# A block-sparse attention and gated FFN kernel: V rows of 96 halves instead of 66, and output slots of 128 words instead of 66

## The chip, the cores and the metric

The kernel runs on one core of one Trainium2 chip. The metric is device time in microseconds (us); a profile's span, from the first to the last recorded instruction, is about 2 us shorter. A run counts as slow when it is over 1.5% above the fastest run of the same kernel; all runs told of here are fast, or are single runs of a kernel (state unknown, since one run has nothing to be compared with).

## The reference, cut to what matters

```
# q, k, v: (4 batches, 8 heads, 768 tokens, 64)
scores = scale * np.matmul(q, k.transpose(0, 1, 3, 2))
scores = np.where(mask, scores, -1000000000.0)          # mask by blocks of 32 tokens
attn = np.exp(scores - max); attn = attn / (sum + 1e-09)
attn_out = np.matmul(attn, v)
x = attn_out as (3072 tokens, 512)
out = (sigmoid(x @ w_gate) * (x @ w_val)) @ w_out       # 512 -> 1536 -> 512
```

(The softmax and sigmoid lines are shortened.) The change concerns `attn @ v` alone.

## The kernel before: the parts that matter

A program of operations is ordered ahead of time by a small scheduler, so each engine gets a fixed list. V is held as eight tiles, each with rows for two heads and six key blocks of 128 keys. A row has 64 values of one key as halves (16-bit floating-point numbers, two bytes each), and then ones: the 65th column of the product is the sum of the weights, by which the output is divided.

```python
VW = 66
...
vring = [one([128, 2, NJ, VW], f16, f"v16_{i}") for i in range(8)]       # NJ = 6
...
lambda i=i: nc.vector.memset(vring[i]()[:, :, :, 64:VW], 1.0),           # the ones, once
...
lambda: nc.vector.tensor_copy(t()[:, :, :, 0:64], s()),                  # cast_v: the values
...
o, rz, x16 = psb([4, VW]), sb("rz", [128, 4, 1], f32), sb("x16", [128, 2, 128], f16)

def values():                                                            # L681 in the profile
    v_ = v16[b, p]()
    for jq in range(2):
        for hd in range(2):
            for j in range(NJ):
                nc.tensor.matmul(
                    o()[:, 2 * jq + hd, 0:65],
                    pts[j // 2]()[:, hd, j % 2, jq * 128 : jq * 128 + 128],
                    v_[:, hd, j, 0:65],
                    start=(j == 0), stop=(j == NJ - 1),
                )
...   # then, on VectorE: L691 rz = 1 / o[:, :, 64:65], L695 x16 = o[:, :, 0:64] * rz
```

`values` is a burst of 24 matmuls, and there are 48 bursts. Each matmul has its own weight load (of `pts`, the exponentials) and streams one row of the V tile, 65 columns, through it. `psb([4, VW])` takes a bank of PSUM, the memory that the products go to, and lays the four output slots of a burst at steps of VW words of four bytes.

The softmax here doesn't subtract the row's maximum and nothing guards it: scores larger than these inputs give would overflow.

## Time and profile before

| what | value | where from |
|---|---|---|
| time | 292.51 us (291.97 to 293.05, four runs) | timed runs |
| TensorE busy | 98% of 290.6 us | table of busy times |
| ScalarE, VectorE busy | 70%, 64% | the same |
| a burst of 24 V matmuls, start to next work | 0.76 us, 31.7 ns a matmul | timeline of PE |
| one of these matmuls in the group table | 193 ns | groups by line |

The last two rows differ because matmuls overlap.

### The profile page before, as it was taken

How to read it: one execution, taken by the hardware profiler on the slowest of the kernel's cores; microseconds unless marked ns; L12 is line 12 of the kernel's file. 1: busy time of each engine (PE TensorE's matmuls, PEld its weight loads, DVE VectorE, ACT ScalarE, POOL GpSimd, SP SyncE). 2: the span in 40 equal slices, each digit the busy share in tenths (PEclk: the TensorE clock that was granted, in tenths of full speed). 3: DMA queues.
4: the chain of work that ended last, by engine and by line, in shares of the span. 5: the costliest groups of instructions: out<-in, count | busy, mean ns of one | idle time of the engine just before them, and what ended most of it. 6: DMA issues, size and time to landing. Idle time of an engine off the chain costs nothing.

```text
span 290.6 us, 7279 instructions
## 1 busy us (share of the span) xinstructions
PE 285.1 (98%) x3030; PEld 175.1 (60%) x3030; DVE 186.5 (64%) x401; ACT 204.4 (70%) x281; POOL 14.8 (5%) x24
## 2 busy tenths in 40 slices
PE   7998999999999999999999999999999999999995
PEld 6676786687578655555554555555555555447753
DVE  3587997898897876867486576476476565223210
ACT  2878888987898898886898796776777673333321
POOL 8740000000000000000000000000000000000000
PEclk9999999999999999999999999999999999999999
DMA  7999998993799973051957651011011011000013
GB/s 106 175 208 210 208 252 229 237 276 65 217 199 210 218 206 64 18 182 25 224 171 165 211 89 56 9 49 54 11 47 54 11 46 56 36 36 35 9 67 111
DMA packets 50785, 35.25 MB, mean 121 GB/s; under 512 B 31376, under 2 KB 47808, under 8 KB 50752
## 3 DMA queue, kind: packets, MB, share of 16 engines
q1 hardware_dynamic: 43304, 27.71, 36.8%
q0 software_dynamic: 7232, 7.01, 15.0%
q8 instruction: 23, 0.38, 0.5%
q10 hardware_dynamic: 216, 0.07, 0.1%
q14 instruction: 10, 0.08, 0.1%
HBM read 28.42 MB, written 6.29 MB: 119 GB/s over the span
## 4 chain that ended last, share of the span: by engine, by line
PE 96%; ACT 2%; DMA 1%; ACTq 0%; issue 0%
PE psum L746 44%; PE psum L791 22%; PE psum L640 14%; PE psum L681 12%; ACT pt L658 1%; PE psum L457 1%; DMA e<-bb_e 1%; PE psum L380 1%; PE psum L720 1%; PE psum L602 1%; PE psum L578 0%; ACTq L353 0%; ACTq L357 0%; ACT y L809 0%; ACTq L658 0%
## 5 line engine op out<-in xcount | busy, mean ns | idle before, releaser
L658 ACT ACTIVATE pt<-psum 128x1024 f16<-128x1024 f32 x144 | 138.9, 1029 | 26.3 <-PE psum L640 26.3
L666 DVE TENSOR_TENSOR pt<-pt,mask 128x1024 f16<-128x1024 f16 x132 | 88.5, 687 | 45.9 <-ACT pt L658 45.8
L746 PE MATMUL psum<-x,wv 128*128 128x256 f16 (+1 forms) x384 | 78.2, 326 | 0.0
L746 PE MATMUL psum<-x,wg 128*128 128x256 f16 (+1 forms) x384 | 78.1, 326 | 0.0
L767 ACT ACTIVATE tg<-psum 128x256 f32<-128x256 f32 (+1 forms) x96 | 47.5, 499 | 42.6 <-PE psum L746 31.8
L791 PE MATMUL psum<-wo,h 128*128 128x512 f16 (+2 forms) x300 | 73.0, 371 | 0.0
L774 DVE SCALAR_TENSOR_TENSOR h<-tg,psum 128x256 f16<-128x256 f32 (+1 forms) x96 | 52.3, 551 | 29.1 <-PE psum L746 16.1
L746 PEld LDWEIGHTS <-wg 128*128 128x128 f16 x384 | 36.0, 98 | 24.3 <-issue 1.7
L746 PEld LDWEIGHTS <-wv 128*128 128x128 f16 x384 | 35.3, 98 | 23.0 <-issue 2.5
L681 PEld LDWEIGHTS <-pt 128*128 128x128 f16 x1152 | 42.5, 98 | 8.8 <-issue 1.1
L640 PE MATMUL psum<-qT,kT 64*128 64x256 f16 x576 | 46.0, 274 | 0.5 <-ACT pt L658 0.4
L791 PEld LDWEIGHTS <-h 128*128 128x128 f16 x300 | 26.4, 98 | 30.2 <-issue 5.7
L681 PE MATMUL psum<-v,pt 128*128 128x65 f16 x1152 | 44.3, 193 | 0.3 <-ACT pt L658 0.3
L640 PEld LDWEIGHTS <-kT 64*128 64x128 f16 x576 | 24.9, 95 | 18.5 <-issue 15.2
L695 DVE TENSOR_TENSOR x<-psum,rz 128x256 f16<-128x256 f32 x48 | 20.4, 424 | 1.8 <-DVE rz L691 0.2
L809 ACT ACTIVATE y<-psum 128x512 f32<-128x512 f32 (+2 forms) x22 | 12.7, 579 | 11.0 <-PE psum L791 10.8
L691 DVE RECIPROCAL rz<-psum 128x4 f32<-128x4 f32 x48 | 8.6, 179 | 5.5 <-PE psum L681 5.4
L380 PE MATMUL psum<-zero 128*64 128x128 f16 x44 | 6.4, 294 | 1.0 <-DVE zero L350 1.0
L640 PE MATMUL psum<-bias,e 64*128 64x256 f16 x48 | 7.1, 307 | 0.0
L427 ACT CAST q<-qs 128x768 f16<-128x768 f32 x8 | 6.8, 844 | 0.0
L610 DVE TENSOR_SCALAR mask<-psum 128x512 f16<-128x512 f32 x9 | 6.0, 683 | 0.5 <-PE psum L640 0.5
L380 PEld LDWEIGHTS <-zero 128*64 128x64 f16 x44 | 4.7, 159 | 2.3 <-issue 1.3
(54 smaller groups left out, 73.1 us busy)
## 6 DMA issues: line engine op xcount, KB each, us to landing
out_dram<-y SPq DMA_DIRECT2D x23, 256.0 KB, 2.0
qs<-in_q_dram SPq DMA_DIRECT2D x12, 384.0 KB, 4.5
vs<-in_v_dram SPq DMA_DIRECT2D x12, 384.0 KB, 4.9
ks<-in_k_dram SPq DMA_DIRECT2D x12, 384.0 KB, 4.4
wg<-in_moe_w_gate_dram POOLq DMA_DIRECT2D x2, 768.0 KB, 13.1
wv<-in_moe_w_val_dram POOLq DMA_DIRECT2D x2, 768.0 KB, 15.8
wo<-in_moe_w_out_dram POOLq DMA_DIRECT2D x3, 512.0 KB, 21.9
vh<-in_v_dram POOLq DMA_DIRECT2D x4, 192.0 KB, 7.7
```

What stands on the lines that cost most here:

```text
L380: "PE", dur, lambda: nc.tensor.matmul(t()[0:64], zero()[:, 0:64], zero(), start=True, stop=True),
L640: nc.tensor.matmul(st()[:, hd, jj * CH : (jj + 1) * CH], l[r, 2 * tt + jj, :], m[r, 2 * c : 2 * c + 2, :], start=not (own and masked), sto ...
L658: lambda st=st, pt=pt: nc.scalar.activation(pt().rearrange("p h j q -> p h (j q)"), st(), AF.Exp, scale=SCALE),
L666: nc.vector.tensor_tensor(t, t, mask()[:, c, tt].unsqueeze(1).to_broadcast([128, 2, 512]), op=ALU.mult)
L681: nc.tensor.matmul(o()[:, 2 * jq + hd, 0:65], pts[j // 2]()[:, hd, j % 2, jq * 128 : jq * 128 + 128], v_[:, hd, j, 0:65], start=(j == 0), ...
L691: "DVE", 0.2, lambda: nc.vector.reciprocal(rz(), o()[:, :, 64:65]), reads=[o], writes=[rz], prio=seq - 5
L695: lambda: nc.vector.tensor_tensor(x16().rearrange("p j (h d) -> p (j h) d", d=64), o()[:, :, 0:64], rz().to_broadcast([128, 4, 64]), op=AL ...
L746: nc.tensor.matmul(t()[:, z : z + w], wt()[:, i, f * 128 : (f + 1) * 128], xT[g, i]()[:, 0:w], start=(i == 0), stop=(i == NP - 1),)
L767: lambda tg=tg, a=pair[0]: nc.scalar.activation(tg()[:, 0:w], a[0]()[:, a[1] : a[1] + w], AF.Tanh, scale=0.5),
L774: lambda tg=tg, a=pair[1], h_=h_: nc.vector.scalar_tensor_tensor(h_()[:, 0:w], tg()[:, 0:w], 1.0, a[0]()[:, a[1] : a[1] + w], op0=ALU.add, ...
L791: nc.tensor.matmul(py()[:, m], hts[g, f]()[:, tt * 128 : (tt + 1) * 128], wo()[:, f, m], start=(f == 0), stop=(f == NF - 1),)
L809: lambda py=py, y=y, m=m: nc.scalar.activation(y()[:, m], py()[:, m], AF.Copy, scale=0.5),
```

## The change

A change of alignment: rows of 96 halves are 192 bytes, so every row starts at a multiple of 64 bytes within its tile; and the four slots of 128 words (512 bytes) lie each on a 512-byte boundary. The whole diff:

```diff
-VW = 66
+VW = 96
...
-            lambda i=i: nc.vector.memset(vring[i]()[:, :, :, 64:VW], 1.0),
+            lambda i=i: nc.vector.memset(vring[i]()[:, :, :, 64:65], 1.0),
...
-        o, rz, x16 = psb([4, VW]), sb("rz", [128, 4, 1], f32), sb("x16", [128, 2, 128], f16)
+        o, rz, x16 = psb([4, 128]), sb("rz", [128, 4, 1], f32), sb("x16", [128, 2, 128], f16)
```

## The prediction

> **What bounds the kernel now.** I read the page's table of busy times first, then the chain that ended last, then the groups by line, then the timeline of one steady stretch, and at the end the start times of single matmuls in the trace. The table of busy times says which engine is full:
>
> ```profile
> PE 285.1 (98%) x3030; PEld 175.1 (60%) x3030; DVE 186.5 (64%) x401; ACT 204.4 (70%) x281; POOL 14.8 (5%) x24
> ```
>
> TensorE (PE) is busy 98% of 290.6 us, and no other engine passes 70%. The chain of work that ended last says whether the end hangs on it:
>
> ```profile
> PE 96%; ACT 2%; DMA 1%; ACTq 0%; issue 0%
> PE psum L746 44%; PE psum L791 22%; PE psum L640 14%; PE psum L681 12%; ACT pt L658 1%; PE psum L457 1%; DMA e<-bb_e 1%; PE psum L380 1%; PE psum L720 1%; PE psum L602 1%; PE psum L578 0%; ACTq L353 0%; ACTq L357 0%; ACT y L809 0%; ACTq L658 0%
> ```
>
> 96% of the span is matmul after matmul on PE. The change touches one line of these, L681, the product of attention weights and values: 12% of the span, about 36 us (the chain in order of time gives 12.5%, 36.3 us). The groups by line show how many such matmuls there are, and what reads their result:
>
> ```profile
> L681 PEld LDWEIGHTS <-pt 128*128 128x128 f16 x1152 | 42.5, 98 | 8.8 <-issue 1.1
> L681 PE MATMUL psum<-v,pt 128*128 128x65 f16 x1152 | 44.3, 193 | 0.3 <-ACT pt L658 0.3
> L695 DVE TENSOR_TENSOR x<-psum,rz 128x256 f16<-128x256 f32 x48 | 20.4, 424 | 1.8 <-DVE rz L691 0.2
> L691 DVE RECIPROCAL rz<-psum 128x4 f32<-128x4 f32 x48 | 8.6, 179 | 5.5 <-PE psum L681 5.4
> ```
>
> 1152 matmuls are 48 bursts of 24: two query halves by two heads by six key blocks. Each needs its own weight load and streams 65 columns of the V tile (64 values and a one that sums the weights). A mean of 193 ns is no cost: 1152 x 193 would be 222 us, and the group is busy for 44.3. What counts is how far apart they start. The timeline of PE in a steady stretch gives that by burst:
>
> ```profile
> 188.56 0.92 PE L681 MATMUL psum<-v,pt 128*128 128x65 f16 x24
> 189.32 1.02 PE L746 MATMUL psum<-x,wv 128*128 128x512 f16 x4
> ...
> 194.07 0.42 PE L681 MATMUL psum<-v,pt 128*128 128x65 f16 x8
> ```
>
> The columns are start, length, engine, line. From the burst's start to that of the next work is 189.32 - 188.56 = 0.76 us, or 31.7 ns a matmul; the whole period is 194.07 - 188.56 = 5.51 us, and PE has no idle time in it. The page's view of stretches agrees: PE is busy 44.2 of 45 us from 15 to 60 us, 50.0 of 50 from 60 to 110, and 134.0 of 134 from 110 to 244.
>
> Then I took the start times of the 24 matmuls of every burst from the trace, and the interval from each to the next, averaged over the 48 bursts. In ns, for matmul 0 to 11 of a burst (12 to 23 repeat it, on the same rows of V):
>
> ```
> 29.9 34.9 32.4 32.5 | 29.1 32.7 32.6 32.7 | 29.2 33.0 32.2 32.6
> ```
>
> One of four takes 29.2, and the other three take 32.7 on average. That is the finding which the prediction rests on. Matmul i streams row i mod 12 of the V tile. A row is 66 halves, 132 bytes, so row i starts 4 x i bytes past a multiple of 16, modulo 16: 0, 4, 8, 12, 0, and so on. The built program places all eight V tiles at addresses that are multiples of 32 (18784, 20384, ...), so exactly the rows 0, 4 and 8 start on a 16-byte boundary, and these are the fast ones.
>
> **What the Trainium skill says.** "TensorE: Matmul & The Clock Gate", section Back-to-back issue gap, gives N / 2.4 + 2.5 ns for a warm matmul of N columns. For 65 columns that is 29.6 ns; the trace has 29.2 for the aligned rows, and 32.7 for the others, which the formula does not have. "SBUF — State Buffer", section Specifications, says that the memory has 16-byte cachelines and that each cross to a new line costs. This fits the period of four rows, though the page gives no figure for a row that starts inside a line, and 130 bytes from an offset of 0, 4, 8 or 12 touch nine lines each. The 3.5 ns is therefore this trace's figure alone. "PSUM — Partial Sum Buffer", section Specifications, gives 8-byte cachelines there. The slots of before start at 0, 264, 528 and 792 bytes, all multiples of 8, so the page promises nothing for the second part of the change. "Perfetto Trace Analysis", section Identifying the Most-Contended Engine, warns that matmul busy time is a bad measure because matmuls are pipelined; hence start intervals and not the 98%.
>
> **The change, part by part.** First, the order of instructions is the same on every engine, with the same waits: the comparison of the two built programs differs only in the shape of eight VectorE memsets. So nothing moves; only durations can change.
>
> (a) Rows of 192 bytes are twelve lines of 16, and the tiles again start at multiples of 32 (18784, 21088, ...). So every row starts on a 16-byte boundary. Must it be 32 or 64? No: before, the fast rows 0, 4 and 8 start at 32, 48 and 0 modulo 64, and take 29.1 to 29.9 alike. So all 24 matmuls of a burst should take 29.2. Of 24, 18 are slow now: 18 x (32.7 - 29.2) = 63 ns a burst. I take this for the last matmul too, though 13 of the 48 bursts end in a switch of about 125 ns that may hide its 3.5. Times 48: 3.0 us of PE time.
>
> (b) Where this lies. From 60 us on PE never idles, and 36 of 48 bursts are there (264 and 600 matmuls in the stretches from 60 to 110 and from 110 to 244 us). They give 36 x 0.063 = 2.3 us, all of it on the path that sets the end. The other 12 bursts lie before 60 us, where the start intervals of PE show some waits, for inputs and for the exponentials (3.4 us beyond the formula between 20 and 40 us, against about 1 in each 20 us later). They hold 0.75 us, of which I take a quarter as lost in those waits: 0.2 us.
>
> (c) The output slots of 128 words in place of 66. Before, slot s holds matmuls 6s to 6s + 5. If the slot's start mattered to the write, the intervals would change every six matmuls. They don't: the fast ones are 29.9 and 29.1 in slot 0, 29.2 in slot 1, and 29.2 in slots 2 and 3. Gain: 0. On VectorE, L691 and L695 read with steps of 512 bytes in place of 264. L695 takes 424 ns for four pieces of 64, and L774 takes 417 for 256 words in one piece, so the pieces cost next to nothing now. Gain: 0.
>
> (d) Eight memsets write 12 separate halves each in place of 24; they take 78 ns each before any data have landed, 0.6 us in all off the path. The casts into V (553 ns on VectorE, 848 on ScalarE, against 553 and 844 for the same cast into q, whose rows are even) have nothing to win. All other SBUF tiles behind V move by 5632 bytes, a multiple of 64. Cost: 0.
>
> Sum: 3.0 - 0.2 = 2.8 us off 292.6, which is **289.8 us**, 1.0% faster.
>
> **The rivals.**
>
> The weight load is the floor: 1152 loads alternate with 1152 matmuls, and if they set the pace, a faster stream gains nothing: 292.6. For it: the trace has a load start 1 to 2 ns after each matmul's start, so they run in lockstep. Against it: the loads all read 256-byte pieces of the same kind of tile, yet the intervals differ by row of V, and six of 24 run at 29.2 with a load each. I give it one in twelve. A milder form, in which the load can keep up with one short interval in four but not with a row of them, would give half: 291.1.
>
> Another engine takes the place of PE early. From 60 to 110 us ScalarE is busy 43.3 of 50 us and VectorE 42.6, so an order fixed in advance may make PE wait there once it runs faster. If the 23 bursts before 110 us gave nothing, 25 x 0.063 = 1.6 us would remain: 291.0. Against it: PE shortens by 0.06 us in some 4 us, 1.5%, and ScalarE has 13% to spare.
>
> The slots do matter, with the cost shared by all of them: each slot of before but the first starts off a 512-byte boundary. Then the gain could pass 3 us, to 289 or below. Nothing in the intervals speaks for it.
>
> **Range and chances.** The point is 289.8. The top of the range, 291.0, holds the mild form of the first rival and the second one; only a full floor by the loads lies above it. The bottom, 289.2, adds the 0.2 us of (b), the extra 2 ns of each burst's second matmul, and the 0.3 us by which runs of before differ. Faster by over 2% needs 5.9 us, twice what all slow intervals hold: 0.02. Slower by over 2% has no mechanism: 0.01. Within 2%: 0.97.
>
> **What would show it.** The intervals of a burst should be 29 ns throughout, 0.70 us from a burst's start to the next work in place of 0.76, and the steady period 5.45 in place of 5.51 us. The mean of L681 should fall by some 3 ns, to 190, with its share of the chain near 11.8%, and L691 and L695 should stay at 179 and 424 ns. A burst still at 0.76 us would make the reading of 16-byte lines wrong. A burst at 0.70 with a span that shrinks by less than 2 us would make (b) wrong, and new idle time of PE before L681 or L640, released by ScalarE, would show where the rest went. A change in L695 would make (c) wrong.

## The result, and the profile after

The changed kernel took 290.35 us (290.32 to 290.92, four runs) against 292.51, with a ratio of 0.9931 and a 95% interval of 0.9908 to 0.9953. A ratio is the mean time of one kernel's fast runs over that of the other's of the same rounds, so it is not quite the ratio of the medians quoted. It is 0.7% faster.

The page of the changed kernel: the busy times, the chain that ended last by line, and the groups of the lines concerned.

```profile
PE 282.4 (98%) x3030; PEld 172.7 (60%) x3030; DVE 186.7 (65%) x401; ACT 204.3 (71%) x281; POOL 14.9 (5%) x24
...
PE psum L746 44%; PE psum L791 23%; PE psum L640 13%; PE psum L681 12%; DMA q<-in_q_dram 2%; ACT pt L658 1%; PE psum L457 1%; PE psum L720 1%; POOL k L439 0%; PE psum L602 0%; POOL k_a L486 0%; POOL q_late L439 0%; POOL q L439 0%; POOL k_b L490 0%; PE psum L380 0%
...
L681 PEld LDWEIGHTS <-pt 128*128 128x128 f16 x1152 | 41.0, 97 | 8.8 <-issue 1.1
...
L681 PE MATMUL psum<-v,pt 128*128 128x65 f16 x1152 | 42.7, 193 | 0.3 <-ACT pt L658 0.3
...
L695 DVE TENSOR_TENSOR x<-psum,rz 128x256 f16<-128x256 f32 x48 | 20.4, 424 | 1.7
...
L691 DVE RECIPROCAL rz<-psum 128x4 f32<-128x4 f32 x48 | 8.6, 179 | 4.9 <-PE psum L681 4.8
```

L681 is busy 42.7 us in place of 44.3, while its mean stays at 193 ns. L695 and L691 take 424 and 179 ns as before, so VectorE got nothing from the new slots. The timeline of PE in a steady stretch (start, length, engine, line):

```profile
186.72 0.89 PE L681 MATMUL psum<-v,pt 128*128 128x65 f16 x24
187.45 1.02 PE L746 MATMUL psum<-x,wv 128*128 128x512 f16 x4
...
192.20 0.47 PE L681 MATMUL psum<-v,pt 128*128 128x65 f16 x10
```

A burst now takes 187.45 - 186.72 = 0.73 us, and the period is 192.20 - 186.72 = 5.48 us: 0.03 less than before, where 0.06 was forecast. The start times of single matmuls in the trace say why. Intervals from matmul 0 to 11 of a burst to the one after it, means over the 48 bursts, in ns:

```
before   29.9 34.9 32.4 32.5 29.1 32.7 32.6 32.7 29.2 33.0 32.2 32.6
changed  30.1 34.7 29.4 29.1 29.5 29.2 34.4 29.3 29.3 29.6 29.9 33.6
```

(The means blur this: where 33.6 stands, most bursts have 35 and the others 29.) The 32.6s are gone, as forecast. But in nearly every burst one interval in five is now 35 ns, which was not. So the average fell from 31.85 to 30.46, not to 29.2. (These two averages are over the 23 intervals inside a burst.) Summed over 48 bursts, the time from a burst's start to the next matmul after it fell from 37.93 to 36.31 us: 1.62 us, about half of the 3.0 forecast.

The span fell by more than that, 290.6 to 288.5. The rest is the start of the program. The first burst begins at 15.29 us in the profile before and at 14.47 in this one. Here are matmuls of the start in the two profiles, which the change does not touch. In the group table (line, engine, shapes, count, busy us and mean ns), before:

```profile
L640 PE MATMUL psum<-bias,e 64*128 64x256 f16 x48 | 7.1, 307 | 0.0
```

and after:

```profile
L640 PE MATMUL psum<-bias,e 64*128 64x256 f16 x48 | 6.0, 273 | 0.0
```

In the profile before, TensorE still ran slow at 9.3 us. Its timeline there:

```profile
8.26 0.42 PE L640 MATMUL psum<-bias,e 64*128 64x256 f16 x2
8.47 0.42 PE L640 MATMUL psum<-qT,kT 64*128 64x256 f16 x2
8.69 0.42 PE L640 MATMUL psum<-bias,e 64*128 64x256 f16 x2
```

The same kind of matmul in the changed kernel's profile:

```profile
6.42 0.27 PE L640 MATMUL psum<-qT,kT 64*128 64x256 f16 x2
6.53 0.27 PE L640 MATMUL psum<-bias,e 64*128 64x256 f16 x2
6.64 0.27 PE L640 MATMUL psum<-qT,kT 64*128 64x256 f16 x2
```

A pair takes 0.21 us in the first and 0.11 in the second, as at half the clock. The trace's own record of the granted clock fits: its entry for the full clock begins at 9.7 us in the first and at 5.6 us in the second (the page's clock line, at 9 from the start, does not show this). Over the twelve profiles of the experiments the first burst began anywhere from 13.96 to 15.37 us, and the slow form (307 ns) came back in one of a kernel with the new behaviour (pitch98, full clock from 9.6 us), so most of this difference is chance. From the first burst to the end, the profiles have 275.33 us before and 274.08 after: 1.25 us. Chance touches this less: a second profile of the changed kernel has 273.83.

### The profile page after: what moved, and what is told of

The parts are those of the page before. It is cut to its first block, busy times and chain, and to the rows that moved or that the text cites. A ratio compares the mean times of both kernels' runs of the same rounds, so it can differ in the third digit from the quotient of the medians.

```text
span 288.5 us, 7279 instructions
## 1 busy us (share of the span) xinstructions
PE 282.4 (98%) x3030; PEld 172.7 (60%) x3030; DVE 186.7 (65%) x401; ACT 204.3 (71%) x281; POOL 14.9 (5%) x24
## 4 chain that ended last, share of the span: by engine, by line
PE 93%; DMA 2%; ACT 2%; POOL 2%; issue 0%; ACTq 0%; POOLq 0%
PE psum L746 44%; PE psum L791 23%; PE psum L640 13%; PE psum L681 12%; DMA q<-in_q_dram 2%; ACT pt L658 1%; PE psum L457 1%; PE psum L720 1%; POOL k L439 0%; PE psum L602 0%; POOL k_a L486 0%; POOL q_late L439 0%; POOL q L439 0%; POOL k_b L490 0%; PE psum L380 0%
## 5 line engine op out<-in xcount | busy, mean ns | idle before, releaser
L746 PE MATMUL psum<-x,wv 128*128 128x256 f16 (+1 forms) x384 | 78.2, 326 | 0.0
L746 PE MATMUL psum<-x,wg 128*128 128x256 f16 (+1 forms) x384 | 78.2, 326 | 0.0
L746 PEld LDWEIGHTS <-wg 128*128 128x128 f16 x384 | 35.9, 98 | 24.3 <-issue 1.7
L746 PEld LDWEIGHTS <-wv 128*128 128x128 f16 x384 | 35.3, 98 | 23.0 <-issue 2.5
L681 PEld LDWEIGHTS <-pt 128*128 128x128 f16 x1152 | 41.0, 97 | 8.8 <-issue 1.1
L640 PE MATMUL psum<-qT,kT 64*128 64x256 f16 x576 | 45.0, 271 | 0.5 <-ACT pt L658 0.4
L681 PE MATMUL psum<-v,pt 128*128 128x65 f16 x1152 | 42.7, 193 | 0.3 <-ACT pt L658 0.3
L640 PEld LDWEIGHTS <-kT 64*128 64x128 f16 x576 | 24.5, 94 | 18.6 <-issue 15.4
L695 DVE TENSOR_TENSOR x<-psum,rz 128x256 f16<-128x256 f32 x48 | 20.4, 424 | 1.7
L691 DVE RECIPROCAL rz<-psum 128x4 f32<-128x4 f32 x48 | 8.6, 179 | 4.9 <-PE psum L681 4.8
L640 PE MATMUL psum<-bias,e 64*128 64x256 f16 x48 | 6.0, 273 | 0.0
```

What stands on the lines that cost most here:

```text
L640: nc.tensor.matmul(st()[:, hd, jj * CH : (jj + 1) * CH], l[r, 2 * tt + jj, :], m[r, 2 * c : 2 * c + 2, :], start=not (own and masked), sto ...
L681: nc.tensor.matmul(o()[:, 2 * jq + hd, 0:65], pts[j // 2]()[:, hd, j % 2, jq * 128 : jq * 128 + 128], v_[:, hd, j, 0:65], start=(j == 0), ...
L691: "DVE", 0.2, lambda: nc.vector.reciprocal(rz(), o()[:, :, 64:65]), reads=[o], writes=[rz], prio=seq - 5
L695: lambda: nc.vector.tensor_tensor(x16().rearrange("p j (h d) -> p (j h) d", d=64), o()[:, :, 0:64], rz().to_broadcast([128, 4, 64]), op=AL ...
L746: nc.tensor.matmul(t()[:, z : z + w], wt()[:, i, f * 128 : (f + 1) * 128], xT[g, i]()[:, 0:w], start=(i == 0), stop=(i == NP - 1),)
```

## The experiments

Twelve kernels ran. In all, PE's order of instructions in the built program is that of the changed kernel (in five traces a few neighbours of the first 27 us start in swapped order), and the results are right except where told. Averages of intervals are over the 23 intervals inside each of 48 bursts.

**Which half of the change does it?** Three kernels in the same rounds, against before at 292.07 us (11 runs).

rows_only undoes the slots:

```diff
-        o, rz, x16 = psb([4, 128]), ...
+        o, rz, x16 = psb([4, 66]), ...
```

> V rows of 192 bytes, output slots at 66 words as before. Theory (row starts): all of the gain, so the bursts look as in the changed kernel: 30.4 ns a matmul (29.2 with one of about 35 in every five), and a time within 0.3 us of the changed kernel, ratio to before 0.993 to 0.997. Rival (slots share the cost): bursts between 30.4 and 31.8 ns, and a gain clearly smaller than that of the changed kernel in the same rounds.

Measured: 290.48 us, ratio 0.9939 (0.9919 to 0.9959), intervals 30.46 ns on average, the long ones at the same places.

slots_only is the kernel before with the new slots alone:

```diff
-        o, rz, x16 = psb([4, VW]), ...
+        o, rz, x16 = psb([4, 128]), ...
```

> V rows of 132 bytes as before, output slots of 128 words. Theory (row starts): no gain, ratio 0.999 to 1.001, bursts at 31.8 ns with the 29, 33, 33, 33 pattern of before. Rival (slots share the cost): a gain of 0.5 us or more and a changed pattern.

Measured: 292.27 us, ratio 1.000 (0.9979 to 1.002), intervals 31.85 ns in the pattern of before.

after_again is the changed kernel without an edit.

> The changed kernel as it is, to measure its gain on the same chip as the two halves, and to get a second profile. The bursts of the first profile are shorter by 1.6 us in all, but its start[...] was also 0.8 us shorter than that of before. If that part is chance, the ratio is 0.994 to 0.996 (1.2 to 1.8 us); if it belongs to the change, 0.992 to 0.993 again.

Measured: 290.59 us, ratio 0.9951 (0.993 to 0.9972), intervals 30.46 ns. The first burst began at 14.58 us, and from there to the end were 273.83 us; slots_only has 275.31. So the rows make all of the gain and the slots none. The gain here is 1.5 us, from the medians; from the first burst on it is 1.25 to 1.50, from the profiles of before and the two of the changed kernel.

**Is it the alignment of the rows?** shift4 keeps the pitch (the distance from one row's start to the next one's) of 192 bytes and moves every row off its 16-byte boundary:

```diff
-            lambda i=i: nc.vector.memset(vring[i]()[:, :, :, 64:65], 1.0),
+            lambda i=i: nc.vector.memset(vring[i]()[:, :, :, 66:67], 1.0),
...
-  t()[:, :, :, 0:64], s()          # in the three casts
+  t()[:, :, :, 2:66], s()
...
-                            v_[:, hd, j, 0:65],
+                            v_[:, hd, j, 2:67],
```

> The changed kernel, with the values two halves (4 bytes) into each 192-byte row, so that all twelve rows of a tile start 4 bytes past a multiple of 16. Theory (row starts): every interval about 32.7 ns and no 29s, 32.7 x 24 x 48 = 37.7 us of starts against 36.5 before, so slower than before by about 1 us, ratio 1.002 to 1.005. Rival (the pitch of 192 bytes is what helps, or the distance between rows): intervals as in the changed kernel, 30.4 on average, ratio 0.995.

Measured: 290.58 us, ratio 0.9934 (0.9912 to 0.9957), intervals 30.08 ns: 29, 32 or 33, 29, 29 and so on. My theory said 32.7 for each; it fell. Rows that all start inside a 16-byte piece are, if anything, faster than aligned ones.

pitch72 has rows of 144 bytes, all on a 16-byte boundary, half of them not on a 32-byte one:

```diff
-VW = 96
+VW = 72
```

> The changed kernel with rows of 72 halves, 144 bytes, nine times 16. Theory (16-byte starts are enough): as the changed kernel, 30.4 ns on average with one 35 in about five, ratio to before 0.994 to 0.996. Rival (a coarser boundary of 32 or 64 bytes is needed): some rows slow, average 31 ns or more.

Measured: 290.38 us, ratio 0.9934 (0.9905 to 0.9963), intervals 30.47 ns. The number alone fits the theory that had just fallen, and also every rival in which the distance of the rows counts; it only excludes a boundary coarser than 16 bytes.

shift8 and shift12 are shift4 with the values 4 and 6 halves into the row:

```diff
-                            v_[:, hd, j, 0:65],
+                            v_[:, hd, j, 4:69],        # shift8; 6:71 in shift12
```

> All rows 8 bytes past a multiple of 16, at the pitch of 192. The run with 4 bytes past it was faster than the aligned rows (30.0 ns on average against 30.4), so the first theory, an own cost for each row that starts inside a 16-byte line, has fallen for 4 bytes. Theory C (a change of offset from one row to the next costs; a constant offset does not): 30.0 to 30.4 ns. Theory R (each offset has its own cost; the kernel before then needs 33 ns for the offsets 8 and 12): about 33 ns.

> All rows 12 bytes past a multiple of 16. Theory C: 30.0 to 30.4 ns on average. Theory R: about 33 ns.

Measured: 30.10 and 30.28 ns, 290.21 and 290.5 us in one run each. None of the four starts within a 16-byte piece that were tried (0, 4, 8 and 12) is slow by itself. What was left: the kernel before changes the offset from row to row (theory C), or something happens between rows that touch each other (theory L). In the kernel before, row 0 ends at byte 129 of the tile and row 1 starts at 132, in the same 16-byte piece (128 to 143). The same holds from row 1 to 2 and from 2 to 3. But row 3 ends at byte 525 and row 4 starts at 528, which begins a new piece. Rows 1, 2 and 3 of each four are the slow ones, and row 4 is not. This also gives the size of the piece: rows 1 and 2 share no piece of 8 bytes (one ends at 261, the other starts at 264), and row 2 is slow; rows 3 and 4 share one of 32 bytes (512 to 543), and row 4 is fast. Two kernels separate the theories.

pitch98 lets the offsets run as before, but keeps the rows apart:

```diff
-VW = 96
+VW = 98
```

> Rows of 98 halves, 196 bytes: the starts run through 0, 4, 8 and 12 bytes past a multiple of 16 as in the kernel before, but a row ends 66 bytes ahead of the next one's start. In the kernel before, the last 16-byte piece of rows 0, 1, 2 is also the first piece of the row that follows it. Theory L (a row that begins in the piece in which the row before ended is slow; rows 1, 2, 3 of each four): no slow rows here, 30.0 to 30.4 ns on average, ratio 0.994 to 0.996. Theory C (the change of offset is slow): as the kernel before, 31.8 ns with the 29, 33, 33, 33 pattern, ratio 0.999 to 1.001.

Measured: 290.38 us, ratio 0.9928 (0.9903 to 0.9954), intervals 30.36 ns. PE in a steady stretch:

```profile
187.39 0.89 PE L681 MATMUL psum<-v,pt 128*128 128x65 f16 x24
188.11 1.03 PE L746 MATMUL psum<-x,wv 128*128 128x512 f16 x4
```

0.72 us a burst, although only one row in four starts on a 16-byte boundary.

pitch64 is the reverse: all rows aligned, each ending in the piece where the next begins. Its result is wrong (the divisor is a constant, and the 65th column is the next row's first value):

```diff
-    vring = [one([128, 2, NJ, VW], f16, f"v16_{i}") for i in range(8)]
+    vring = [one([128, 13 * 64], f16, f"v16_{i}") for i in range(8)]     # memset of 768:832
...
-                            v_[:, hd, j, 0:65],
+                            v_[:, (hd * NJ + j) * 64 : (hd * NJ + j) * 64 + 65],
...
-  nc.vector.reciprocal(rz(), o()[:, :, 64:65])
+  nc.vector.tensor_scalar(rz(), o()[:, :, 0:1], 0.0, 1.0 / S, op0=ALU.mult, op1=ALU.add)
```

> Wrong result on purpose: rows of exactly 64 halves, 128 bytes, of which the matmul reads 65, the last being the first half of the next row; the divisor is a constant. All rows start on a 16-byte boundary, and each one's last piece is the first piece of the next row. Theory L: every row but the first of a query half is slow, about 32.5 ns on average, 37.4 us of starts. Theory C, and the first theory of aligned starts: 30.4 ns as in the changed kernel.

Measured: 292.69 us in one run (before: 292.25 in the same rounds), intervals 32.37 ns. PE in a steady stretch:

```profile
188.64 0.94 PE L681 MATMUL psum<-v,pt 128*128 128x65 f16 x24
189.41 1.02 PE L746 MATMUL psum<-x,wv 128*128 128x512 f16 x4
```

0.77 us a burst, a little worse than before. The means over all bursts, matmul 0 to 12:

```
pitch98  30.1 34.5 29.3 29.5 29.3 31.7 29.4 29.4 29.2 33.9 29.3 29.7 29.2
pitch64  30.0 34.9 32.7 32.4 32.6 32.4 32.6 32.4 32.6 32.4 32.6 32.4 29.1
```

In pitch64 all intervals are slow but that of matmul 0 and of matmul 12, which goes back to row 0 after row 11 and so shares nothing with the row ahead of it. The pieces that matmul 12 reads were all read twelve matmuls earlier, so it is the read just ahead that counts. (Matmul 1 takes 32.6 to 34.9 ns in all kernels with 65 columns.) In pitch98, look at rows 2 and 3 of each four: 29.3 to 29.8 ns, where the kernel before has 32.2 to 32.7. Row 1 of each four proves nothing there: it stays at 31.7 to 34.5, but so it does in shift4 (32.2 to 32.6), where nothing touches and no offset changes; these are the long intervals that come next. Theory L said 32.5 and no slow rows, and holds in both; theory C and the alignment theory said the opposite and fall in both.

**Why is one interval in five long?** cols64 streams 64 columns, so the sum is missing and the result is wrong:

```diff
-                            o()[:, 2 * jq + hd, 0:65],
+                            o()[:, 2 * jq + hd, 0:64],
...
-                            v_[:, hd, j, 0:65],
+                            v_[:, hd, j, 0:64],
...                          # the constant divisor of pitch64
```

> Wrong result on purpose: the matmuls of the changed kernel stream 64 columns, without the one; the divisor is a constant. Asks why one interval in five is 35 ns. Theory (pairs of weight load and matmul have a pace of their own, 30.4 ns on average): the intervals between the long ones fall to 28.8, but the average stays near 30.4, so the long ones come more often. Rival (the moving read delivers 16 bytes at a time, and 65 halves need a ninth piece for one element): no long intervals, 28.8 ns throughout. Third (a matmul here or there is simply late by 5.8 ns, one in five): average 28.8 + 1.2 = 30.0, still one in five.

Measured: at every place a mean of 29.1 to 29.2, on average 29.16 ns, no 35s; one run, 289.57 us. The pace-of-the-pairs theory said 30.4 and falls.

cols32 does the same with 0:32, each column used twice:

> Wrong result on purpose: 32 columns, each used twice; the divisor is a constant. Theory (pace of the pairs): the average stays near 30.4 ns[...]. Rival (the moving read): the average falls clearly, to 25 or less.

Measured: 25.0 ns for every interval after the first (average 25.16); 284.55 us in one run. PE in a steady stretch:

```profile
187.76 0.75 PE L681 MATMUL psum<-v,pt 128*128 128x32 f16 x24
188.37 1.02 PE L746 MATMUL psum<-x,wg 128*128 128x512 f16 x4
```

24 weight loads and matmuls in 188.37 - 187.76 = 0.61 us. So the weight load can keep up with 25 ns, and by itself is not what holds the bursts at 30.

cols66 streams 66 columns, two of them ones, with a right result:

```diff
-            lambda i=i: nc.vector.memset(vring[i]()[:, :, :, 64:65], 1.0),
+            lambda i=i: nc.vector.memset(vring[i]()[:, :, :, 64:66], 1.0),
...                          # and 0:66 in the two operands of the matmul
```

> The changed kernel, streaming 66 columns, the last two both ones; the result is right. With 64 columns no interval was long. Theory (an odd count leaves the one lone element in the ninth 16-byte piece of a row, and a lone element costs): no long intervals, a steady 30.0 ns, which is less than the 30.4 of 65 columns; the time 0.3 to 0.4 us below the changed kernel, ratio 0.993 to 0.995. Rival (any ninth piece costs): an average of 30.8 ns or more, with long intervals.

Measured: 290.89 us, ratio 0.9956 (0.9921 to 0.9991); steady bursts at 30.43 ns with the same long intervals, 30.51 over all bursts. So the odd count is not the cause, and no gain is to be had that way. Adding a 66th column costs nothing to speak of (30.51 against 30.46), removing the 65th gives 1.3 ns. That fits a cost of the ninth 16-byte piece, but the rival with that name asked for 30.8 or more, and with other starts in the piece the long intervals change (32 or 33 in one of four in shift4). What exactly makes them stays open.

No version clearly beats the changed kernel. shift4 and shift8 have the shortest bursts, 35.85 and 35.87 us in all against 36.31, but the times cannot tell 0.5 us apart: ratios 0.9934 for shift4 and pitch72, with intervals of 0.004 and more.

## Why the prediction was right in the time and wrong in the cause

**The time** fell within the range: 290.35 against 289.8, with 289.2 to 291.0, and within 2%. A part of this is luck. The forecast was a gain of 2.8 us, 1.6 at the upper end of the range. The first rounds gave 2.2, of which the profiles put 0.8 into a start that the change does not touch; the later rounds gave 1.5 (292.07 to 290.59), just short of that end. That PE sets the end, that the order does not move, and that start intervals and not lengths are to be read, held. In the range itself there is a slip: it was to hold the milder form of the first rival, but that form's 291.1 lies above 291.0.

**Step (a), the reading of the slow rows, failed.** It said that "exactly the rows 0, 4 and 8 start on a 16-byte boundary, and these are the fast ones". True, but rows 0, 4 and 8 differ from the others in a second way: they begin in a 16-byte piece that the row ahead of them did not end in. With a pitch of 132 bytes the two always go together, and the profile before could not separate them. The runs did: aligned and touching is slow (pitch64, 32.4 ns), not aligned and not touching is fast (pitch98, 30.4; shift4, 30.1). The change helps because it moves the rows apart. The prediction had a warning in hand: it counted nine 16-byte lines for a row at any of the four offsets, so that alignment gave a row nothing less to read. Why a shared piece costs time is not shown by any run.

**Its size failed too.** Of the 18 slow intervals counted, 16 inside a burst did go from 32.6 to 29.2, which is 16 x 3.4 = 54 ns; the burst's second one stayed at 35. But some four more long ones came, at 5.8 ns each, 4 x 5.8 = 23; kernels whose rows touch have few of these but the second. The net is 31 ns a burst and, with the interval at its end, 1.62 us in all, not 3.0. The assumption "all 24 matmuls of a burst should take 29.2" is the term that was off. The milder form of the first rival gave this size (half), but for a wrong reason: the weight load keeps up with 25 ns in cols32.

**Step (b)** asked that bursts after 60 us count in full and some 0.2 us be lost before. From the first burst on, 1.25 to 1.50 us of 1.62 reached the end: 0.1 to 0.4 lost. The first half held to the letter: from the 13th burst (at 64.8 us before) to the 48th, both profiles of the changed kernel gain 1.17 us, 33 ns a burst, all that the bursts are shorter by. The 0.25 us between these two profiles lie elsewhere: 0.15 at 58.4 us, where eight matmuls of L640 take 0.70 us to the next work (0.54 before and in after_again), and 0.1 after the last burst. What PE waited for there is not known. The period fell by 0.035 us (from 5.515 to 5.480, averaged over the steady bursts).

**Step (c), the slots give nothing**, held: slots_only at 1.000, and L691 and L695 at their old lengths.

**Step (d)** held: the memsets take 68 in place of 78 ns each, though the eight together 0.49 in place of 0.30 us, off the path.

**What it expected of the profile:** L681's mean should have fallen to 190 ns; it stayed at 193: the recorded length does not follow the spacing (cols64 has 193 too, at 29.16 ns from start to start). A burst at 0.70 us was expected and 0.73 came.

**What it left out** is the start. The first rounds' 2.2 us contain a start that differs by up to 1.4 us between profiles of kernels alike there. Timed runs of kernels with bursts of 30.1 to 30.5 ns are 1.1 (cols66) to 2.2 us (pitch72) below before of their rounds, by medians. The best estimate for the change is about 1.5 us, from the later rounds and from the profiles after the first burst.

## What to carry to other kernels

Before you give a pattern a cause, look for a second property that the fast cases share; here alignment and touching rows went together, and one kernel for each corner (aligned but touching, apart but not aligned) told them apart in two runs. Where short matmuls stream successive rows of a packed tile, leave a gap so that no row begins in the 16-byte piece in which the last one ended: a pitch of 72 halves did here as much as 96. And do not forecast that all will run at the pace of the fastest when the profile has only single fast ones among slow ones.

## What the Trainium skill lacked or had wrong

- "SBUF — State Buffer", section Specifications, has 16-byte cachelines and a penalty for each cross to a new one. It lacks what these runs show: a matmul whose moving row begins in the 16-byte piece in which the row of the matmul ahead ended is followed by the next start after 32.4 to 32.6 ns, where most others take 29.2 (65 columns of fp16; on average over a burst 32.37 in pitch64 against 30.08 to 30.47 in the kernels whose rows do not touch); where rows start within a piece makes little difference (30.08 to 30.46 ns on average for 0, 4, 8 and 12 bytes).
- "TensorE: Matmul & The Clock Gate", section Back-to-back issue gap: the formula N / 2.4 + 2.5 gives 29.17 ns for 64 columns, and 29.16 was measured. The section's table, which puts 1 to 64 columns at a floor of about 25 ns, agrees at 32 columns (25.0) but not at 64. For 65 columns the formula gives 29.6, and the best average was 30.08, made of 29s and one longer interval in four or five. No page has these.
- The same section says that streams of weight load and matmul sustain about 81 ns a matmul at N = 128 and 131 at N = 512, and that its formula is for a matmul by itself (the prediction left this out). Here such pairs took 25.0 ns with 32 columns, 29.16 with 64, 55 or 56 with 128 (14 of the 24 matmuls of L720 in the profile before; the other ten 66 or more) and 216 with 512 (L746, 0.86 us for four): from 64 columns on near the formula, and far from both figures.
- "PSUM — Partial Sum Buffer", section Specifications, has 8-byte cachelines but says nothing of what the start of an output costs. Slots at multiples of 264 bytes cost nothing against 512 (ratio 1.000, 0.9979 to 1.002); both are multiples of 8, and no run has slots that are not.
